# Weight groups' due times, batch 3's transposes and the last 256 tokens' down phase in an attention and two-MLP kernel

## Chip, core and metric

The kernel runs on one core of one Trainium2 chip. The metric is the device time of a run in microseconds (us), as the median over several runs.

## What is computed

The inputs are `x` (8 batches × 8 heads × 512 tokens × 64) and `state` (8 × 8 × 32 × 64), the weights of two MLPs, and the gain `g_ln`. Matrices and results are float32. Cut to what matters:

```python
xread, sread = attention(x -> state), attention(state -> x)      # both ways, per batch and head
y = concat([xread, sread], axis=2)           # 8 x (512 + 32) tokens of 512
# first MLP: W_in 512 x 1024, W_out 1024 x 512
h = y @ moe_w_in
e = exp(h - h.max(-1)); solu = h * e / (e.sum(-1) + 1e-9)
ln = (solu - mean) / sqrt(var + 1e-6) * g_ln
x2 = ln @ moe_w_out
# second MLP: W_in 512 x 2048, W_out 2048 x 512
h = x2 @ moe2_w_in
out = (h * sigmoid(1.702 * h)) @ moe2_w_out
```

## The kernel before, in words

The program has two halves. In the first, attention and the first MLP run batch by batch (8 batches of 512 tokens; the 256 state tokens come as a ninth, smaller batch). In the second, the second MLP runs its up half over all batches and then its down half over all batches. Between the halves the tokens (`x2`) go through DRAM.

Products are made with float32 split into a high and a low part: each full product is three TensorE instructions (hi × hi, lo × hi, hi × lo; lines 422, 423 and 424 in the first MLP, 1010 to 1012 and 1089 to 1091 in the second).

**Transposes.** TensorE contracts over partitions, so tokens have to be turned. Per batch there are two sorts of it. The x transposes turn x for the state's scores (the products on line 571). In `x_T` TensorE turns a block against the identity into PSUM (line 543) and another engine copies it out. In `x_T_dma` four transfers on SyncE lay x out in SBUF so that one VectorE transpose in 32 × 32 blocks (line 533) finishes the work. `XD` is the first batch that takes the second way. The z transposes turn the normalised hidden block `u` for the first MLP's second product. In `z_T` TensorE does it (line 827) and ScalarE and VectorE make the high and low part from PSUM (line 835 for the low part). In `z_turn` VectorE transposes blocks of half the hidden width (line 797, into `zw`), sixteen transfers on SyncE bring them into place (`z`), and ScalarE and VectorE make the two parts in SBUF (line 816 for the low part). From batch `ZB` on, the second half of a batch's hidden width is turned in that way.

**Seven products in place of eight.** The second MLP multiplies 2 × 2 blocks by the scheme with seven products P1 to P7. Its factors are sums of blocks. For the weights, `prepare_up` does it for one group of four blocks (`w3_kq..`; k and q are 0 or 1). `to_f32` first turns raw 64-bit weights into float32 by a chain of integer and float instructions on ScalarE, VectorE (lines 444, 447, 449) and GpSimd (line 451, 1.4 us each). `sums` then makes four sums on VectorE (line 880, names a1 to a4). Seven splits into high and low parts follow (`hi_w3s..`, `lo_w3s..`), and fourteen transfers to DRAM. Four such groups are needed before the up half starts. Three of them are given due times of 205, 255 and 310; the fourth follows later. For the down half `factors_down` loads four blocks of the hidden layer for batch c and makes four sums and seven splits of them. The last 256 tokens are done differently: `down_plain` takes the four plain products with two blocks, one sum and three splits, for two halves of 128 tokens, 192 products of 256 columns in all (lines 1135 to 1137). Then two evacuations of 512 columns (the last one on line 1143) and four stores follow.

**What sets the order.** No engine's order is written out by hand. Every step is handed to a planner (class `Plan`) with a cost, and some with a due time (`key`); a due time goes back along the dependences to the steps ahead of it. The planner simulates the engines and lists each engine's steps: among those that can start, TensorE takes the one with the smallest key and the others the one with the smallest due time. So a smaller due time moves a whole group of steps ahead of others on VectorE, ScalarE, GpSimd and SyncE. Steps that write a new tile wait for a free slot of the tile's kind, and nearly all transfers are issued by SyncE in one order.

Of the kernel before, what the change touches and what calls it, by code (L numbers as in the profile page):

```python
# [343 lines left out]
def attention_solu_gelu(ctx: ExitStack, tc: tile.TileContext, x, state, w1, w2, g_ln, w3, w4, out):  # L344
# [774 lines left out]
    def down_plain(base):  # L1119

        acc = [tl("m", [P, 512], F32, f"W{u}") for u in range(2)]
        gs = [factors_down(B, j, base + j * 4 * PP) for j in range(NM // 2)]
        dst = out.rearrange("(b t) e -> b t e", t=T)
        nb = P // NS
        for u in range(2):
            for j in range(NM // 2):
                for n, (f, i, gi) in enumerate(((0, P1, 0), (0, P2, 1), (1, P7, 0), (1, P3, 2))):
                    def go(e, j=j, n=n, f=f, i=i, gi=gi, u=u):
                        hi, lo = gs[j][gi]
                        o = acc[u]()[:, 256 * f:256 * f + 256]  # L1130
                        cut = slice(u * P, u * P + P)
                        for mi in range(2):
                            wt = W4[i, 2 * j + mi]()
                            first = not j and not mi and not n
                            nc.tensor.matmul(o, hi()[:, mi, cut], wt[:, 0], start=first, stop=False, **OPEN)  # L1135
                            nc.tensor.matmul(o, hi()[:, mi, cut], wt[:, 1], start=False, stop=False, **OPEN)  # L1136
                            nc.tensor.matmul(o, lo()[:, mi, cut], wt[:, 0], start=False, stop=2 * j + mi == NM - 1 and n == 3, **OPEN)  # L1137
                    do(PE(PP / 2), go, [*gs[j][gi], W4[i, 2 * j], W4[i, 2 * j + 1]], [acc[u]],
                       base + (u * 8 + j * 2 + n / 2) * PP)
            o = tl("s", [P, DM], F32, f"os{u}")  # L1140
            due = base + 8 * (u + 1) * PP
            if u:
# [124 lines left out]
```

## Time and profile before

| | before |
|---|---|
| median of 3 runs | 1137.73 us (1136.8 to 1139.35) |
| the profiled execution | 1138.69 us |
| its span in the trace | 1136.9 us |
| TensorE products busy | 1091.8 us, 96% |
| VectorE busy | 811.9 us, 71% |
| ScalarE busy | 636.8 us, 56% |
| GpSimd busy | 257.7 us, 23% |
| granted TensorE clock, mean | 0.984 of full speed |

The span is what the trace covers of an execution. Busy shares are means over the whole program, and it has stages of different kinds: attention and the first MLP up to about 450 us (their last tokens some 25 us longer), then the up half of the second MLP to about 790 us, its down half to the end. Which engine is waited for has to be read stage by stage, from stretches. The granted clock says at what share of full speed TensorE was allowed to run.

### The profile page before, as it was taken

To read this page: it belongs to the slowest core of one execution; us is meant where nothing else is said; L and a number is where in the kernel's file an instruction comes from. 1 tells how busy PE (TensorE), PEld (TensorE's weight loads), DVE (VectorE), ACT (ScalarE), POOL (GpSimd) and SP (SyncE) were. 2 spreads that over 40 slices of the span, in tenths; PEclk is the share of its full clock that TensorE was granted. 3 is DMA by queue.
4 is the path that set the end of the run, shared out by engine and by line. 5 is a ranking of instruction groups with operands and counts; after the bars stand their busy time and mean duration, and the time that the engine had idled before them with its cause. 6 is when DMAs were issued, how large, how long until landed. Compare 5 with 4: busy or idle time off the path is not lost.

```text
span 1136.9 us, 21706 instructions
## 1 busy us (share of the span) xinstructions
PE 1091.8 (96%) x8111; PEld 987.6 (87%) x8111; DVE 811.9 (71%) x1370; ACT 636.8 (56%) x1168; POOL 257.7 (23%) x219
## 2 busy tenths in 40 slices
PE   6799899998999999999999999999999999999998
PEld 2467677776676789999999999999999999999998
DVE  6999677499879946728857755635488888778870
ACT  6686655865867646637756665645244444344430
POOL 3865352455548510501111001000000000000000
PEclk8999899999999999999999999999999999999999
DMA  8213133328663649998677667459944254334511
GB/s 250 56 40 110 40 60 85 104 51 261 135 192 129 194 90 358 350 360 292 232 239 239 240 214 256 175 207 398 383 144 123 66 176 138 119 123 149 178 55 47
DMA packets 216185, 200.67 MB, mean 177 GB/s; under 512 B 111888, under 2 KB 157968, under 8 KB 216080
## 3 DMA queue, kind: packets, MB, share of 16 engines
q1 hardware_dynamic: 215984, 199.16, 55.1%
q8 instruction: 63, 1.03, 0.4%
q14 instruction: 42, 0.34, 0.1%
q10 hardware_dynamic: 96, 0.13, 0.0%
HBM read 112.20 MB, written 82.84 MB: 172 GB/s over the span
## 4 chain that ended last, share of the span: by engine, by line
PE 57%; DVE 1%; DMA 1%; POOL 0%; issue 0%; ACT 0%; POOLq 0%; DVEq 0%; ACTq 0%
PE psum L1089 9%; PE psum L1090 9%; PE psum L1091 9%; PE psum L1010 9%; PE psum L1011 9%; PE psum L1012 9%; PE psum L1137 1%; PE psum L1057 1%; PE psum L1136 1%; PE psum L1058 1%; PE psum L1056 1%; PE psum L1135 1%; DMA w3k_1l<-lo_w3s 0%; DVE lo_x L957 0%; DMA w3k_1h<-hi_w3s 0%
## 5 line engine op out<-in xcount | busy, mean ns | idle before, releaser
L1089 PE MATMUL psum<-w4r,hi_g 128*128 128x256 f32 x896 | 251.8, 281 | 1.7 <-DVE oc L1100 1.7
L1090 PE MATMUL psum<-w4r,hi_g 128*128 128x256 f32 x896 | 251.6, 281 | 0.0
L1091 PE MATMUL psum<-w4r,lo_g 128*128 128x256 f32 x896 | 251.4, 281 | 0.0
L1089 PEld LDWEIGHTS psum<-w4r,hi_g 128*128 128x128 f32 x896 | 169.1, 189 | 1.8 <-ACT hi_g L463 1.8
L1091 PEld LDWEIGHTS psum<-w4r,lo_g 128*128 128x128 f32 x896 | 169.2, 189 | 0.0
L1090 PEld LDWEIGHTS psum<-w4r,hi_g 128*128 128x128 f32 x896 | 169.0, 189 | 0.0
L463 ACT CAST hi_g<-a_g 128x512 fp32r<-128x512 f32 x124 | 75.2, 620 | 120.4 <-DVE a_g L880 79.5
L451 POOL TENSOR_TENSOR w_w<-w_w,raw_w 128x512 uint32<-128x512 uint32 x48 | 68.8, 1439 | 283.7 <-DVE w_w L449 152.4
L422 PE MATMUL psum<-zhi,hi_w 128*128 128x512 f32 (+1 forms) x288 | 116.7, 405 | 2.8 <-DVE zlo L835 1.3
L1022 DVE TENSOR_TENSOR c<-psum,u 128x512 f32<-128x512 f32 x64 | 44.1, 690 | 98.5 <-PE psum L1012 63.8
L424 PE MATMUL psum<-zhi,lo_w 128*128 128x512 f32 (+1 forms) x288 | 111.7, 388 | 0.0
L957 DVE TENSOR_TENSOR lo_g<-a_g,hi_g 128x512 fp32r<-128x512 f32 x128 | 83.8, 685 | 18.3 <-PE psum L1090 9.5
L994 ACT ACTIVATE t<-c 128x512 f32<-128x512 f32 x96 | 60.5, 633 | 51.1 <-DVE c L1022 49.5
L423 PE MATMUL psum<-zlo,hi_w 128*128 128x512 f32 (+1 forms) x224 | 85.7, 382 | 0.1
L957 DVE TENSOR_TENSOR lo_g<-gr,hi_g 128x512 fp32r<-128x512 f32 x104 | 70.8, 684 | 11.0 <-ACT hi_g L463 9.2
L463 ACT CAST hi_g<-gr 128x512 fp32r<-128x512 f32 x104 | 61.4, 618 | 28.2 <-PE psum L1090 14.5
L422 PEld LDWEIGHTS psum<-zhi,hi_w 128*128 128x128 f32 x288 | 55.4, 192 | 19.5 <-issue 4.1
L424 PEld LDWEIGHTS psum<-zhi,lo_w 128*128 128x128 f32 x288 | 55.5, 193 | 11.6
L1010 PE MATMUL psum<-hi_x,w3r_1h 128*128 128x256 f32 x224 | 63.0, 281 | 1.2 <-ACT u L1017 1.2
L1011 PE MATMUL psum<-lo_x,w3r_3h 128*128 128x256 f32 x224 | 63.0, 281 | 0.0
L1011 PE MATMUL psum<-lo_x,w3r_2h 128*128 128x256 f32 x224 | 63.0, 281 | 0.0
L1011 PE MATMUL psum<-lo_x,w3r_0h 128*128 128x256 f32 x224 | 63.0, 281 | 0.0
(256 smaller groups left out, 3104.2 us busy)
## 6 DMA issues: line engine op xcount, KB each, us to landing
g<-t SPq DMA_DIRECT2D x136, 256.0 KB, 2.9
gr<-g SPq DMA_DIRECT2D x136, 256.0 KB, 3.5
w4r<-w4k SPq DMA_DIRECT2D x56, 256.0 KB, 5.2
raw_w<-in_moe_w_in SPq DMA_DIRECT2D x24, 512.0 KB, 5.4
...
```

Of the source, the lines that this page charges most:

```text
L422: nc.tensor.matmul(o, lhi, rhi, start=first, stop=False)
L423: nc.tensor.matmul(o, lhi, rlo, start=False, stop=False)
L424: nc.tensor.matmul(o, llo, rhi, start=False, stop=last)
L451: do(POOL(1.23), lambda e: e.tensor_tensor(u(), u(), raw()[:, :, 0], op=ALU.add), [w, raw], [w], key=due)
L463: e.copy(o, i)
L957: do(DVE(.68), lambda e: e.tensor_tensor(flat_(lo), flat_(t), flat_(hi), op=ALU.subtract), [t, hi], [lo], key=due)
L1010: nc.tensor.matmul(o, wh()[:, k, cut], hi()[:, k, :], start=first and not mi + k, stop=False, **OPEN)
L1011: nc.tensor.matmul(o, wh()[:, k, cut], lo()[:, k, :], start=False, stop=False, **OPEN)
L1012: nc.tensor.matmul(o, wl()[:, k, cut], hi()[:, k, :], start=False, stop=bool(mi and k), **OPEN)
L1089: nc.tensor.matmul(o, hi()[:, mi, cut], wt[:, 0], start=first, stop=False, **OPEN)
L1090: nc.tensor.matmul(o, hi()[:, mi, cut], wt[:, 1], start=False, stop=False, **OPEN)
L1091: nc.tensor.matmul(o, lo()[:, mi, cut], wt[:, 0], start=False, stop=2 * j + mi == NM - 1 and u == 1, **OPEN)
```

## The change

Three things change.

**Batch 3 goes over to the second way of transposing.** `ZB` and `XD` fall from 4 to 3. Batch 3's x transposes are now sixteen transfers and four VectorE transposes; the second half of its z transposes is four VectorE transposes, sixteen transfers and the two parts made in SBUF. TensorE loses 16 transposes of x and 16 of u.

**Two weight groups get smaller due times:** 205 and 255 become 160 and 230. The third keeps 310.

**The last 256 tokens' down phase** takes seven products instead of four times two. `factors_down` now makes four half-size sums for each of four steps j (in tiles `s` and `r`) and four splits, and `down_last` runs 7 × 4 × 6 = 168 products of 256 columns. The results are combined by half-size evacuations, each of which adds an earlier one, as `finish` does it for the other batches. The stores of 128 tokens go out when P4 is in; the other four follow P3.

```diff
-ZB = 4
-XD = 4
+ZB = 3
+XD = 3
...
-            prepare_up(k, q, (205, 255, 310)[n])
+            prepare_up(k, q, (160, 230, 310)[n])
...
-            parts = sums("a", g, f"g{c}_{j}")
-        else:
-            d = tl("s", [P, 512], F32, f"gd{j}")
-            do(SUM, lambda e: e.tensor_tensor(d(), g[0](), g[1](), op=ALU.add), g, [d])
-            parts = [*g, d]
-        return [split2(t, f"g{c}_{j}{i}", None) for i, t in enumerate(parts)]
+            return [split2(t, f"g{c}_{j}{i}", None) for i, t in enumerate(sums("a", g, f"g{c}_{j}"))]
+        s, r = (tl("s", [P, 512], F32, f"gs{i}_{j}") for i in range(2))
...
+        def two(o, i, x, y, op):
+            do(DVE(.4), lambda e: e.tensor_tensor(cut(o, i), cut(*x), cut(*y), op=op), [x[0], y[0]], [o])
+        two(s, 0, (g[0], 1), (g[1], 1), ALU.add)
+        two(r, 0, (s, 0), (g[0], 0), ALU.subtract)
+        two(s, 1, (g[0], 1), (g[0], 0), ALU.subtract)
+        two(r, 1, (g[1], 0), (r, 0), ALU.subtract)
+        return [split2(t, f"g{c}_{j}{i}", None) for i, t in enumerate((*g, s, r))]
...
-    def down_plain(base):
...
+    def down_last(base):
+        gs = [factors_down(B, j, base) for j in range(NM // 2)]
+        place = {P1: (0, 0), P2: (1, 0), P3: (3, 1), P4: (1, 1), P5: (2, 0), P6: (3, 0), P7: (2, 1)}
...
+        order = ((P1, 0), (P6, 1), (P7, 2), (P5, 3), (P2, 4), (P4, 5), (P3, 6))
+        for i, n in order:
+            if not n % 2:
+                acc[n // 2] = tl("m", [P, 512], F32, f"E{n // 2}")
             for j in range(NM // 2):
...
+                do(PE(PP / 2), go, [*gs[j][place[i][0]], W4[i, 2 * j], W4[i, 2 * j + 1]], [acc[n // 2]],
+                   base + (n * 4 + j) * PP / 2)
...
+        x1 = half(P1, None, "px1")
+        u1 = half(P6, x1, "pu1")
+        u2 = half(P7, u1, "pu2")
+        half(P5, u2, None, (1, 1))
+        u3 = half(P5, u1, "pu3")
+        half(P2, x1, None, (0, 0))
+        half(P4, u2, None, (1, 0))
+        store(1)
+        half(P3, u3, None, (0, 1))
+        store(0)
...
-    down_plain(base)
+    down_last(base)
```

Three places show how the order moves. The names end in batch and block numbers: `xn3_0` is block 0 of batch 3's x, `u1_2` block 2 of batch 1's hidden layer, `xT` and `stT` are turned x and state, `v`, `hi_v` and `lo_v` a product of weights and state, `ahi` attention weights.

TensorE, where batch 3's x is transposed (about 119 to 129 us); before:

```order
L423 MATMUL psum_69<-zlo0_7_1267,hi_w2_7_1294 128x512
L424 MATMUL psum_69<-zhi0_7_1247,lo_w2_7_1306 128x512
L543 MATMUL psum_69<-ident_79,xn3_0_1120 128x128 x4
L543 MATMUL psum_69<-ident_79,xn3_1_1138 128x128 x4
L543 MATMUL psum_69<-ident_79,xn3_2_1163 128x128 x4
L543 MATMUL psum_69<-ident_79,xn3_3_1187 128x128 x4
L827 MATMUL psum_69<-ident_79,u1_0_910 128x128
L827 MATMUL psum_69<-ident_79,u1_1_937 128x128
L827 MATMUL psum_69<-ident_79,u1_2_1058 128x128
L827 MATMUL psum_69<-ident_79,u1_3_1228 128x128
```

After:

```order
L423 MATMUL psum_69<-zlo0_7_1247,hi_w2_7_1289 128x512
L424 MATMUL psum_69<-zhi0_7_1234,lo_w2_7_1301 128x512
L571 MATMUL psum_69<-xT3_1_1308,stT3_948 64x512
L571 MATMUL psum_69<-xT3_0_1299,stT3_948 64x512
L422 MATMUL psum_69<-hi_v2_0_0_1323,ahi2_0_1266 128x512
L423 MATMUL psum_69<-lo_v2_0_0_1327,ahi2_0_1266 128x512
L424 MATMUL psum_69<-hi_v2_0_0_1323,alo2_0_1279 128x512
L422 MATMUL psum_69<-hi_v2_0_1_1386,ahi2_0_1266 128x512
L423 MATMUL psum_69<-lo_v2_0_1_1399,ahi2_0_1266 128x512
L424 MATMUL psum_69<-hi_v2_0_1_1386,alo2_0_1279 128x512
L827 MATMUL psum_69<-ident_79,u1_0_910 128x128
L827 MATMUL psum_69<-ident_79,u1_1_937 128x128
```

The four steps on line 543 are gone, and two score steps of batch 3 and six products of batch 2 stand ahead of u1's transposes instead.

VectorE at about 200 to 210 us, in batch 4's attention, where `w_w3_00ij` are blocks of the first weight group and `zw3` is the block of batch 3's z being turned; before:

```order
L602 RECIPROCAL z1_4_1_2162<-z1_4_1_2162 128x16
L783 TENSOR_SCALAR sml3_2_2063<-sml3_2_2063 128x1
L606 STREAM_TRANSPOSE aT4_1_2198<-s1_4_1_2109 128x512
L533 STREAM_TRANSPOSE xT5_2_2212<-xb5_2_2187 128x512
L533 STREAM_TRANSPOSE xT5_3_2220<-xb5_3_2189 128x512
L465 CAST ahi4_1_2234<-aT4_1_2198 128x512
L641 TENSOR_SCALAR sr4_2299<-psum_69,r2_4_0_2008 128x128
L641 TENSOR_SCALAR sr4_2299<-psum_69,r2_4_1_2112 128x128
```

After:

```order
L602 RECIPROCAL z1_4_1_2215<-z1_4_1_2215 128x16
L444 TENSOR_SCALAR w_w3_0000_2193<-w_w3_0000_2193 128x512
L447 TENSOR_SCALAR w_w3_0000_2193<-w_w3_0000_2193 128x512
L444 TENSOR_SCALAR w_w3_0001_2202<-w_w3_0001_2202 128x512
L449 SCALAR_TENSOR_TENSOR w_w3_0000_2193<-raw_w3_0000_2098,w_w3_0000_2193 128x512
L447 TENSOR_SCALAR w_w3_0001_2202<-w_w3_0001_2202 128x512
L606 STREAM_TRANSPOSE aT4_1_2257<-s1_4_1_2124 128x512
L797 STREAM_TRANSPOSE zw3_1_1989<-u3_2_2090 128x512
L880 TENSOR_TENSOR a2_w3_00_2274<-a1_w3_00_2168,w_w3_0000_2193 128x512
L880 TENSOR_TENSOR a3_w3_00_2283<-w_w3_0010_1998,w_w3_0000_2193 128x512
L465 CAST ahi4_1_2292<-aT4_1_2257 128x512
L533 STREAM_TRANSPOSE xT5_0_2328<-xb5_0_2104 128x512
```

Five conversion steps and two sums of the first weight group, and one transpose of batch 3's z, stand among batch 4's steps; before, the group came later.

VectorE near 388 us, where `z6` is batch 6's z, `u7` and `sml7` batch 7's hidden layer and its small values, and `w3..01` the third weight group; before:

```order
L449 SCALAR_TENSOR_TENSOR w_w3_0101_4073<-raw_w3_0101_4022,w_w3_0101_4073 128x512
L880 TENSOR_TENSOR a2_w3_01_4109<-a1_w3_01_3984,w_w3_0100_4060 128x512
L816 SCALAR_TENSOR_TENSOR z6_1_3900<-z6_1_3900,g_sb_81,zhi6_5_4058 128x4x128
L775 SCALAR_TENSOR_TENSOR u7_3_4104,sml7_3_4088<-psum_69,u7_3_4104 128x1024
L880 TENSOR_TENSOR a3_w3_01_4132<-w_w3_0110_3822,w_w3_0100_4060 128x512
L880 TENSOR_TENSOR a4_w3_01_4139<-w_w3_0101_4073,a2_w3_01_4109 128x512
L780 TENSOR_SCALAR sml7_2_4020<-sml7_2_4020 128x1
L780 TENSOR_SCALAR sml7_3_4088<-sml7_3_4088 128x1
L458 TENSOR_TENSOR lo_w3s6_01_4155<-a3_w3_01_4132,hi_w3s6_01_4142 128x512
L816 SCALAR_TENSOR_TENSOR z6_1_3900<-z6_1_3900,g_sb_81,zhi6_6_4081 128x4x128
L816 SCALAR_TENSOR_TENSOR z6_1_3900<-z6_1_3900,g_sb_81,zhi6_7_4090 128x4x128
```

After:

```order
L775 SCALAR_TENSOR_TENSOR u7_2_4065,sml7_2_4042<-psum_69,u7_2_4065 128x1024
L816 SCALAR_TENSOR_TENSOR z6_1_3921<-z6_1_3921,g_sb_81,zhi6_4_4076 128x4x128
L816 SCALAR_TENSOR_TENSOR z6_1_3921<-z6_1_3921,g_sb_81,zhi6_5_4086 128x4x128
L780 TENSOR_SCALAR sml7_2_4042<-sml7_2_4042 128x1
L797 STREAM_TRANSPOSE zw7_1_4116<-u7_0_3900 128x512
L458 TENSOR_TENSOR lo_w3s4_01_4126<-a1_w3_01_3906,hi_w3s4_01_3991 128x512
L771 TENSOR_REDUCE sml7_3_4132<-psum_69 128x1
L816 SCALAR_TENSOR_TENSOR z6_1_3921<-z6_1_3921,g_sb_81,zhi6_6_4112 128x4x128
L783 TENSOR_SCALAR sml7_2_4042<-sml7_2_4042 128x1
L816 SCALAR_TENSOR_TENSOR z6_1_3921<-z6_1_3921,g_sb_81,zhi6_7_4118 128x4x128
L775 SCALAR_TENSOR_TENSOR u7_3_4145,sml7_3_4132<-psum_69,u7_3_4145 128x1024
```

The sums a2 to a4 of the third group no longer stand here; z6_4 to z6_7 now stand ahead of u7_3.

After about 402 us every engine has the same rows in the same order as before, up to the last phase.

## Rows read from the trace of the kernel before

**Rows 1.** Stretches of the span: length, busy us (instructions) by engine, granted clock, DMA.

```profile
50.00:119.00 69.00, 64.56 (x417) 46.80 (x416) 65.91 (x114) 55.66 (x107) 44.94 (x38) 0.98 0.22 62
119.00:129.00 10.00, 6.55 (x28) 5.44 (x27) 6.92 (x14) 5.42 (x9) 6.00 (x7) 0.66 0.31 114
129.00:240.00 111.00, 110.29 (x640) 84.05 (x640) 75.57 (x146) 68.54 (x134) 39.21 (x38) 1.00 0.29 68
240.00:265.00 25.00, 24.26 (x179) 19.43 (x178) 24.50 (x46) 19.50 (x42) 17.79 (x14) 1.00 0.58 141
265.00:328.00 63.00, 57.59 (x301) 42.53 (x300) 54.13 (x95) 43.97 (x82) 30.63 (x28) 0.95 0.70 178
328.00:401.00 73.00, 67.81 (x352) 51.84 (x351) 64.38 (x106) 48.47 (x93) 51.41 (x42) 0.98 0.56 167
401.00:475.00 74.00, 73.56 (x488) 66.70 (x486) 45.88 (x74) 43.93 (x77) 16.41 (x13) 1.00 0.83 268
475.00:1110.00 635.00, 632.61 (x5352) 632.23 (x5353) 433.56 (x703) 319.30 (x564) 23.82 (x17) 1.00 0.61 206
1110.00:1137.00 27.00, 22.93 (x195) 22.72 (x193) 1.38 (x2) 0.60 (x1) 0.00 (x0) 0.97 0.14 39
```

**Rows 2.** In order of time: start, us, instruction [idle before it <- releaser].

```profile
121.44 2.59 PE L543 MATMUL psum<-ident,xn 128*128 128x128 f32 x12 [1.88 <-DVE xs L465]
125.60 1.09 PE L827 MATMUL psum<-ident,u 128*128 128x128 f32 x4 [1.57 <-DVE xT L465]
133.98 1.08 PE L571 MATMUL psum<-xT,stT 128*64 128x512 f32 x4
...
123.03 1.70 DVE L786 TENSOR_SCALAR u<-u,sml 128x1024 f32<-128x1024 f32 x1 [1.40 <-POOL sml L785]
```

**Rows 3.** Line 533 (xT): duration ns min/median/max, first and last start.

```profile
L533 DVE STREAM_TRANSPOSE xT<-xb x16: 666/700/711, 159.6 to 331.1; 128x512 f32<-128x512 f32 x16
```

**Rows 4.** TensorE in order of time, around four transposes of batch 3.

```profile
225.58 0.39 PE L424 MATMUL psum<-zhi,lo_w 128*128 128x512 f32 x1
225.81 0.60 PE L827 MATMUL psum<-ident,u 128*128 128x128 f32 x4
226.17 0.48 PE L422 MATMUL psum<-hi_v,ahi 128*128 128x512 f32 x1
226.49 0.39 PE L423 MATMUL psum<-lo_v,ahi 128*128 128x512 f32 x1
```

**Rows 5.** Two shorter stretches, columns as in rows 1.

```profile
194.45:220.07 25.62, 25.50 (x179) 19.96 (x177) 14.11 (x34) 21.84 (x42) 13.44 (x12) 1.00 0.28 56
390.00:396.00 6.00, 5.26 (x16) 4.19 (x17) 6.00 (x10) 3.23 (x7) 4.72 (x4) 0.72 0.65 242
```

**Rows 6.** Instructions that touch w_w alone, in two stretches, columns as in rows 1.

```profile
248.00:276.00 28.00, 0.00 (x0) 0.00 (x0) 12.20 (x16) 4.45 (x7) 9.68 (x7) 0.99 0.83 251
312.00:346.00 34.00, 0.00 (x0) 0.00 (x0) 11.58 (x17) 3.82 (x6) 8.14 (x6) 0.99 0.63 183
```

**Rows 7.** Line 880 (block sums): duration ns min/median/max, first and last start.

```profile
L880 DVE TENSOR_TENSOR a_g<-gr,gr x64: 678/683/694, 760.9 to 1085.1; 128x512 f32<-128x512 f32 x64
L880 DVE TENSOR_TENSOR a_w<-w_w,a_w x4: 685/1456/1786, 269.0 to 472.5; 128x512 f32<-128x512 f32 x4
```

**Rows 8.** All engines in order of time, at the wait before 390.74.

```profile
388.47 1.66 POOL L451 TENSOR_TENSOR w_w<-w_w,raw_w 128x512 uint32<-128x512 uint32 x1 [0.63 <-DVE w_w L449]
388.92 1.77 DVE L816 SCALAR_TENSOR_TENSOR z<-z,g_sb,zhi 128x512 fp32r<-128x512 f32 x1
390.74 0.50 PE L423 MATMUL psum<-z,hi_w 128*128 128x512 f32 x1 [2.23 <-DVE z L816]
```

**Rows 9.** Line 1137 (last phase): duration ns min/median/max, first and last start.

```profile
L1137 PE MATMUL psum<-w4r,lo_g x64: 276/282/288, 1110.3 to 1132.7; 128*128 128x256 f32 x64
```

**Rows 10.** All engines in order of time, the span's end.

```profile
1132.97 0.69 DVE L1143 TENSOR_SCALAR os<-psum 128x512 f32<-128x512 f32 x1 [21.98 <-PE psum L1137]
1133.69 0.78 SPq L1149 DMA_DIRECT2D out<-os  x2
```

More of the change, by code (lines that the diff above doesn't have):

```diff
@@ L1117, in finish @@
         store(half(P3, u3, "oc12_"), 0, 1)
-    def down_plain(base):
-        acc = [tl("m", [P, 512], F32, f"W{u}") for u in range(2)]
-        gs = [factors_down(B, j, base + j * 4 * PP) for j in range(NM // 2)]
+    def down_last(base):
+        gs = [factors_down(B, j, base) for j in range(NM // 2)]
+        place = {P1: (0, 0), P2: (1, 0), P3: (3, 1), P4: (1, 1), P5: (2, 0), P6: (3, 0), P7: (2, 1)}
+        acc = {}
         dst = out.rearrange("(b t) e -> b t e", t=T)
         nb = P // NS
-        for u in range(2):
-            for j in range(NM // 2):
[L1127 to L1142, printed above, removed]
-                do(DVE(.6), lambda e, o=o, u=u: e.tensor_scalar(o(), acc[u](), 1 / 1.702, None, op0=ALU.mult), [acc[u]], [o],
-                   key=due)
-            else:
-                do(ACT(.5), lambda e, o=o, u=u: e.activation(o(), acc[u](), AF.Copy, scale=1 / 1.702), [acc[u]], [o], key=due)
-            for q in range(nb):
-                def go(e, o=o, u=u, q=q):
-                    e.dma_start(out=dst[u * nb + q, S:T, :], in_=o()[q * NS:(q + 1) * NS, :])
-                do(ACT(.1) if u and q % 2 else DMA(), go, [o], [], key=due + 20, nbytes=P * 512)
@@ new lines, in down_last, with part, go @@
+        o = [tl("s", [P, 2, 256], F32, f"os{u}") for u in range(2)]
+        def part(n, i):
+            n_, c = divmod(n, 2)
+            return acc[n_]()[:, 256 * c:256 * c + 256]
+        order = ((P1, 0), (P6, 1), (P7, 2), (P5, 3), (P2, 4), (P4, 5), (P3, 6))
+        for i, n in order:
+            if not n % 2:
+                acc[n // 2] = tl("m", [P, 512], F32, f"E{n // 2}")
+            for j in range(NM // 2):
+                def go(e, i=i, n=n, j=j):
+                    t, u = place[i]
+                    hi, lo = gs[j][t]
+                    cut = slice(u * P, u * P + P)
+                    for mi in range(2):
+                        wt = W4[i, 2 * j + mi]()
+                        last = j == NM // 2 - 1 and mi == 1
+                        nc.tensor.matmul(part(n, i), hi()[:, mi, cut], wt[:, 0], start=not (j or mi or n % 2), stop=False, **OPEN)
+                        nc.tensor.matmul(part(n, i), hi()[:, mi, cut], wt[:, 1], start=False, stop=False, **OPEN)
+                        nc.tensor.matmul(part(n, i), lo()[:, mi, cut], wt[:, 0], start=False, stop=last, **OPEN)
+                do(PE(PP / 2), go, [*gs[j][place[i][0]], W4[i, 2 * j], W4[i, 2 * j + 1]], [acc[n // 2]],
+                   base + (n * 4 + j) * PP / 2)
@@ new lines, in down_last, with half, view @@
+        places = dict(order)
+        due = base + 14 * PP
+        def half(i, t, name, to=None):
+            n = places[i]
+            if to is None:
+                w = tl("s", [P, 256], F32, name)
+                dst_ = w
+            else:
+                w, dst_ = o[to[0]], None
+            def view():
+                return dst_() if dst_ is not None else w()[:, to[1]]
+            if t is None:
+                do(ACT(.3), lambda e: e.activation(view(), part(n, i), AF.Copy, scale=1 / 1.702), [acc[n // 2]], [w], key=due)
+            else:
+                do(DVE(.4), lambda e: e.scalar_tensor_tensor(out=view(), in0=part(n, i), scalar=1 / 1.702, in1=t(),
+                                                             op0=ALU.mult, op1=ALU.add), [acc[n // 2], t], [w], key=due)
+            return w
@@ new lines, in store, with go @@
+        def store(u):
+            for q in range(nb):
+                def go(e, q=q):
+                    e.dma_start(out=dst[u * nb + q, S:T, :], in_=o[u]()[q * NS:(q + 1) * NS].rearrange("p a e -> p (a e)"))
+                do(ACT(.1) if not u and q % 2 else DMA(), go, [o[u]], [], key=due + 20, nbytes=P * 512)
+        x1 = half(P1, None, "px1")
[4 more added lines that the diff above has]
+        half(P2, x1, None, (0, 0))
```

2 lines of the change are left out of this document (added).

## The prediction, made before the changed kernel ran

> **What bounds the kernel now.** The first view to read is the table of stretches [rows 1]. Its columns after the length are busy time on TensorE's products, its weight loads, VectorE, ScalarE and GpSimd, then the granted clock. From 401 us on TensorE is busy 706 of 709 us up to 1110 us: whatever VectorE does there is hidden, and time falls only if TensorE gets less to do. Ahead of 401 us it is idle 4.4 us of 69 up to 119 us, 3.5 of 10 at 119 to 129, only 0.7 of 111 up to 240, then 0.7 of 25, 5.4 of 63 and 5.2 of 73. In those last three VectorE is busy 98%, 86% and 88% of the time: TensorE waits for VectorE there. The clock is a second price: a granted 0.66 over 10 us is 3.4 us of lost full-speed time, 0.95 over 63 us is 3.2, 0.98 over 73 us is 1.5.
>
> The instruction order shows a rigid end: from about 402 us on, every engine has the same rows in the same order until the last phase. So a microsecond won ahead of 402 us arrives at the end whole, and a microsecond lost does too. The sum is made against the profiled execution, 1138.69 us (span 1136.9), which is 0.96 us above the median of the runs; I apply it to the median, 1137.73.
>
> **1. The last 256 tokens' down phase.** Before, 192 products run from 1110.3 us; the 64 of one line start 22.4 us apart, first to last [rows 9], so a product takes 22.4 / 63 / 3 = 0.1185 us. Seven products of 4 × 6 are 168, 24 fewer: −2.84 us. The last evacuation before the stores took 0.69 us for 512 columns [rows 10]; the changed one has 256, which I put at 0.42 (an estimate, between half and all): −0.27. VectorE gets sixteen half-size sums for four whole ones, and four more splits, some 6 us in all; it is idle 21.98 us ahead of that evacuation [rows 10], and the inputs are loaded before the phase begins. So the sums hide. If they came late, at the worst the whole gain would go. **−3.1 (−3.1 to 0).**
>
> **2. Batch 3's x transposes, 119 to 129 us.** TensorE waits 1.88 us for VectorE at 121.44, runs twelve transposes for 2.59, waits 1.57 at 125.60, and runs the transposes of u1 [rows 2]. In the changed order the x transposes are gone. Ahead of u1 stand two of the score rows (four instructions, 1.08 us, [rows 2]) and six 512-column products, which follow one another in 0.23 us as [rows 4] has it: 2.5 us of work that came later before. What ends the wait then is the normalisation of u1_3 on VectorE, which ended at 123.03 + 1.70 = 124.73 [rows 2]. Ahead of it VectorE gets up to four of the new transposes, 0.70 each [rows 3], and one 0.68 us subtraction more, and it loses 1.67 us of other work: 0 to 1.8 us later. So u1's transposes start at 124.7 to 126.5 instead of 125.60, with 2.5 us already done: a gain of 1.6 to 3.4. The sixteen transfers on SyncE go ahead of others in its queue, but the DMA engines are busy 0.31 here [rows 1]. What could take the gain away is the clock, 0.66 in this stretch: if it falls again and lasts longer, nothing is left. **−2.0 (−3.4 to 0).**
>
> **3. Half of batch 3's z transposes.** They lie in the stretch of 129 to 240 us, where TensorE is 99% busy, so their time counts whole. Four of them took from 225.81 to 226.17 = 0.36 us, and the product behind them came 0.09 us later than its neighbours (0.32 for 0.23) [rows 4]. Four such groups go: 4 × 0.45 = **−1.8 (−1.8 to −1.4)**. VectorE gets four transposes of 0.70 instead and is busy 75.57 of 111 us there [rows 1]; the sixteen transfers find DMA engines busy 0.29. If that cover failed, TensorE would wait for z, which belongs to the next term.
>
> **4. The first weight group into 187 to 222 us.** Its due time falls from 205 to 160, and its instructions move from about 250 to 274 us to among those of 187 to 222. VectorE's share of a group is 16 to 17 instructions, 12.20 or 11.58 us [rows 6]. The stretch that takes it, 194.45 to 220.07, is 25.62 us long and TensorE is busy 25.50 of them; VectorE is busy 14.11 [rows 5]. Added: 12.5 for the group, 2.1 for three z transposes; gone: two instructions of some 0.7 that move elsewhere, 1.4. That makes 14.1 + 12.5 + 2.1 − 1.4 = 27.3 us where 25.6 are there. One end is no cost, since what does not fit can slide into the relieved stretch behind. The other is 2.0 of overflow, as much again for waits in the order on GpSimd and ScalarE, and one fall of the clock (1.7, as 0.72 over 6 us gives it [rows 5]): 5.7. I take the overflow, since the share of VectorE is what the rows show. **+2.0 (0 to +5.7).**
>
> **5. 240 to 265 us.** Relieved of that group's start, VectorE is no longer busy 24.50 of 25 us [rows 1]; TensorE's idle time there goes. **−0.7 (−0.7 to 0).**
>
> **6. 265 to 328 us.** The rest of the first group leaves, some 6 us, and the second group (due 255 to 230, from 312 to 344 us to among 267 to 300) comes in with 11.6: VectorE from 54.13 to some 59.7 of 63. TensorE is idle 5.4 us. Nothing in the rows says which waits vanish. Below, the lost clock of 3.2 us could come back; above, one more wait as that at 390.74 with its clock would cost 3.9. **0 (−3.2 to +3.9).**
>
> **7. 328 to 401 us.** The second group is gone from here: VectorE falls from 64.38 to about 53 to 59 of 73 (something of the third group draws closer). The longest wait is 2.23 us at 390.74, for batch 6's z, whose low part took 1.77 us beside a GpSimd instruction on a weight block and stood behind the third group's sums [rows 8]. The clock after it was 0.72 over 6 us, 1.7 us lost [rows 5]. In the changed order two of those sums stand earlier, and z6's parts stand ahead of u7_3. I take that one wait with its clock, 2.23 + 1.7. The far end is the stretch's whole idle time and lost clock, 5.2 + 1.5; the near end is 1 us, if another z is late next. **−3.9 (−6.7 to −1.0).**
>
> **Sum.** −3.1 − 2.0 − 1.8 + 2.0 − 0.7 + 0 − 3.9 = −9.5, that is 1137.7 − 9.5 = **1128.2 us**. All terms at their best give −18.9, about 1119; all at their worst +7.2, about 1145.
>
> **Rivals.** *The stalls only move.* VectorE does no less in all; weight sums taken from 312 to 344 us are done in stretches that are full too. Then term 4 comes out at its far end, 3.7 more than in the sum, and term 6 at +3.0, a wait and most of a fall of the clock: 1128.2 + 6.7 = about **1134.9**. For it: VectorE 86 to 98% busy around 240 to 401 [rows 1]. Against: VectorE is idle 35 of the 111 us from 129 to 240. Chance 0.20.
>
> *Slower: the group's two-input operations stretch beside GpSimd.* The weight sums of line 880 took 1456 ns in the middle and 1786 at most, where the same form later takes 683 [rows 7]. GpSimd is busy 13.44 of the 25.62 us of term 4's stretch before anything is added [rows 5], and a group adds 8 to 10 us to it [rows 6]. If nine VectorE instructions there take 1 us more each (0.8 to 1.1 by those rows), VectorE needs 36.3 us in 25.6: TensorE waits 10.7 and loses 1.7 to the clock, 12.4 instead of 2.0. The same in term 6 adds 3.9 + 1.7, term 7's gain staying: 1128.2 + 10.4 + 5.6 = about **1144**. It decides once VectorE's work in that stretch passes some 33 us, where terms 1 to 3 are eaten. Against it: a group's 12.20 and 11.58 us already hold such stretching, with GpSimd busy 9.68 of 28 us on the group itself [rows 6]. Chance 0.08. The Trainium skill, "SBUF — State Buffer", section "Who interferes with whom", has a rule for this: a VectorE instruction with two inputs in SBUF contends with a GpSimd instruction that reads SBUF, and one of them blocks. The rows agree (1456 to 683 ns for one form); by that rule alone each such instruction would wait for a whole GpSimd one, 1.66 us [rows 8], and this rival would be the forecast.
>
> *The waits of 265 to 328 us go too.* Terms 6 at −3.2 and 7 at −6.7: 1128.2 − 6.0 = about **1122**. For it: the order there is looser for z. Against: VectorE has more to do there. Chance 0.12.
>
> *The last phase gives nothing*, its sums coming late for the second product, which starts 24 × 0.1185 = 2.8 us into the phase: **1131.3**. Chance 0.05.
>
> **How the numbers follow.** The forecast has 0.55. The range leaves out the slower rival, half of the first's upper edge and the deepest part of the third: 1121 to 1136. A measurement of this kernel can tell 0.2%, 2.3 us, from no change. The forecast, the third and the fourth rival are faster; of the first rival's 0.20, 0.06 falls within 0.2%. So faster 0.86, same 0.06, slower 0.08.
>
> **What would show it.** In the profile of the changed kernel: products of the last phase ending about 19.9 us after they start (term 1); TensorE's idle time in 119 to 129 us under 2 us (2); VectorE's busy time between about 190 and 215 us near the length of that stretch, with TensorE's idle time there of 0 to 2 us (4), while well over 2 means the slower rival; no wait of over 2 us for z ahead of the stretch that answers to 401 (7). The start of the rigid part should come about 6 us earlier, and the last phase 3 more. The forecast is wrong if TensorE's idle time and lost clock between 129 and 401 us don't fall by some 2 us net.

## The result, and the profile after

The changed kernel took 1125.66 us (median of 6 runs, 1124.97 to 1129.33); the kernel before, run beside it, 1138.11. The ratio is 0.9899, with a 95% interval of 0.9885 to 0.9913: 11.5 us less, by 9.9 to 13.1. The forecast was 1128.2 us, 9.5 less, in a range of 1121 to 1136. So the number was right. The experiments show that most of its terms were not.

The page of the changed kernel: busy time and share of the span of TensorE and VectorE, in a span of 1124.3 us (before 1136.9).

```profile
PE 1080.0 (96%) x8055; PEld 976.9 (87%) x8055; DVE 825.2 (73%) x1398; ACT 637.8 (57%) x1171; POOL 258.7 (23%) x218
```

TensorE was busy 1091.8 us before, so its idle time is 1136.9 − 1091.8 = 45.1 us before and 1124.3 − 1080.0 = 44.3 after. **The waits as a whole hardly shrank.** What shrank is TensorE's busy time, by 11.8 us. To see where, I cut both traces at the same instructions of TensorE. In the rows, `u` is a hidden block, `sml` its small values, `e2t` the exponentials of the state's scores and `sr` the state's scaled result, per batch. First the kernel before: start and end of the stretch, its length, busy us of TensorE's products, its weight loads, VectorE, ScalarE, GpSimd, the granted clock, DMA.

```profile
117.25:138.57 21.32, 17.87 (x80) 13.88 (x80) 15.10 (x26) 11.20 (x20) 8.55 (x9) 0.84 0.15 54
138.57:194.54 55.97, 55.38 (x327) 42.58 (x325) 40.29 (x80) 31.35 (x64) 20.46 (x21) 1.00 0.32 68
194.54:228.75 34.21, 34.09 (x219) 25.96 (x217) 19.66 (x39) 27.33 (x51) 13.62 (x12) 1.00 0.41 107
253.94:280.12 26.18, 22.64 (x97) 16.34 (x94) 24.30 (x34) 16.61 (x29) 16.97 (x13) 0.93 0.87 273
280.12:327.46 47.34, 44.72 (x255) 33.79 (x253) 40.18 (x78) 35.57 (x66) 22.24 (x21) 0.96 0.64 143
327.46:399.10 71.64, 66.44 (x346) 50.78 (x345) 64.21 (x106) 49.01 (x94) 50.15 (x40) 0.98 0.58 171
```

The same stretches of the changed kernel:

```profile
118.52:134.53 16.01, 13.96 (x63) 10.05 (x64) 13.05 (x27) 11.39 (x20) 9.33 (x10) 1.00 0.28 91
134.53:190.32 55.79, 55.22 (x326) 42.66 (x325) 41.45 (x75) 32.82 (x67) 19.61 (x20) 1.00 0.32 77
190.32:231.21 40.89, 35.03 (x220) 25.94 (x218) 38.00 (x64) 30.88 (x58) 26.60 (x21) 1.00 0.63 179
256.08:275.89 19.81, 19.81 (x96) 15.33 (x94) 15.05 (x26) 13.48 (x24) 5.77 (x6) 1.00 0.90 205
275.89:324.91 49.02, 43.62 (x256) 32.48 (x253) 45.06 (x78) 36.92 (x68) 26.96 (x21) 1.00 0.67 175
324.91:388.91 64.00, 63.84 (x347) 49.94 (x345) 55.44 (x98) 44.41 (x90) 43.94 (x36) 1.00 0.49 136
```

By these pairs: −5.3 us where batch 3's x is turned, −0.2 in the next stretch, **+6.7 where the first weight group now lies**, −6.4 where it lay, +1.7, and −7.6 in the last. The stretch left out here (229 to 254 us before) gives −0.3. From then on the order is the same, and the trace is 10 us ahead up to the last phase, which adds 2.9. VectorE's busy time shows the move: 19.66 to 38.00 us in the third pair, 24.30 to 15.05 in the fourth.

In the third stretch TensorE, idle 0.1 us before, now waits 5.9. The largest of these waits, in order of time (start, us, instruction, [idle before it <- releaser]):

```profile
199.04 0.50 PE L422 MATMUL psum<-hi_w1s,sthi 128*128 128x512 f32 x1 [1.71 <-DVE zlo L835]
212.36 0.51 PE L422 MATMUL psum<-hi_w1s,sthi 128*128 128x512 f32 x1 [2.13 <-DVE sr L641]
222.17 0.33 PE L827 MATMUL psum<-ident,u 128*128 128x128 f32 x1 [1.46 <-POOL u L786]
```

And VectorE's instructions of the first group there run long (groups of that stretch: busy us, mean ns | idle before):

```profile
L465 DVE CAST hi_w3s<-w_w 128x512 fp32r<-128x512 f32 x3 | 3.5, 1162 | 0.0
L458 DVE TENSOR_TENSOR lo_w3s<-w_w,hi_w3s 128x512 fp32r<-128x512 f32 x2 | 2.3, 1155 | 0.0
L880 DVE TENSOR_TENSOR a_w<-a_w,w_w 128x512 f32<-128x512 f32 x1 | 1.8, 1759 | 0.0
L465 DVE CAST hi_w3s<-a_w 128x512 fp32r<-128x512 f32 x2 | 0.8, 424 | 0.0
```

One cast form takes 1162 ns on the mean where its like takes 424, and a sum 1759 where [rows 7] has 683 for the plain case. The planner that set this order counts a low part (line 458) at 0.6 us on VectorE, whatever runs beside it.

The span's end, which answers to [rows 10]: the last evacuation has half the columns and takes 0.42 us, as estimated.

```profile
1120.41 0.42 DVE L1174 SCALAR_TENSOR_TENSOR os<-psum,pu 128x256 f32<-128x256 f32 x1 [2.09 <-PE psum L1155]
1120.87 0.89 ACTq L1181 DMA_DIRECT2D out<-os  x2
```

### The profile page after: what moved, and what is told of

It is laid out like the page before. It is cut to its first block, busy times and chain, and to the rows that moved or that the text cites. A ratio compares the mean times of both kernels' runs of the same rounds, so it can differ in the third digit from the quotient of the medians.

```text
span 1124.3 us, 21689 instructions
## 1 busy us (share of the span) xinstructions
PE 1080.0 (96%) x8055; PEld 976.9 (87%) x8055; DVE 825.2 (73%) x1398; ACT 637.8 (57%) x1171; POOL 258.7 (23%) x218
## 4 chain that ended last, share of the span: by engine, by line
PE 75%; DVE 13%; issue 3%; SPq 3%; POOL 3%; DMA 2%; ACT 1%; DVEq 0%; POOLq 0%; ACTq 0%
PE psum L1098 9%; PE psum L1100 9%; PE psum L1099 9%; PE psum L1010 9%; PE psum L1011 9%; PE psum L1012 9%; PE psum L422 5%; PE psum L423 5%; PE psum L424 4%; DVE w_w L449 1%; DVE w_w L444 1%; SPq L529 1%; POOL lo_w3s L458 1%; DVE w_w L447 1%; DVE u L775 1%
## 5 line engine op out<-in xcount | busy, mean ns | idle before, releaser
L422 PE MATMUL psum<-zhi,hi_w 128*128 128x512 f32 (+1 forms) x288 | 113.9, 395 | 1.3 <-DVE zlo L835 0.6
L957 DVE TENSOR_TENSOR lo_g<-gr,hi_g 128x512 fp32r<-128x512 f32 x104 | 71.0, 685 | 11.8 <-ACT hi_g L463 9.2
L423 PE MATMUL psum<-zlo,hi_w 128*128 128x512 f32 (+1 forms) x208 | 78.3, 376 | 0.2
L424 PEld LDWEIGHTS psum<-zhi,lo_w 128*128 128x128 f32 x288 | 54.1, 188 | 11.8 <-DVE lo_w L458 0.4
L1010 PE MATMUL psum<-hi_x,w3r_2h 128*128 128x256 f32 x224 | 63.0, 281 | 0.0
```

What stands on the lines that cost most here:

```text
L422: nc.tensor.matmul(o, lhi, rhi, start=first, stop=False)
L423: nc.tensor.matmul(o, lhi, rlo, start=False, stop=False)
L424: nc.tensor.matmul(o, llo, rhi, start=False, stop=last)
L957: do(DVE(.68), lambda e: e.tensor_tensor(flat_(lo), flat_(t), flat_(hi), op=ALU.subtract), [t, hi], [lo], key=due)
L1010: nc.tensor.matmul(o, wh()[:, k, cut], hi()[:, k, :], start=first and not mi + k, stop=False, **OPEN)
```

## Experiments

Twelve kernels, each against the kernel before on the same chip. Since the median of the kernel before moved between 1136.0 and 1138.1 us from one session to the next, differences are taken from the ratios (a thousandth is 1.14 us).

| kernel | median us | ratio to before (95%) | us against before |
|---|---|---|---|
| the change | 1125.66 | 0.9899 (0.9885 to 0.9913) | −11.5 |
| e1, last phase alone | 1133.83 | 0.9973 (0.9959 to 0.9988) | −3.1 |
| e2, batch 3's transposes alone | 1139.83 | 1.0027 (1.0017 to 1.0037) | +3.1 |
| e3, due times alone | 1138.89 | 1.0014 (1.0003 to 1.0025) | +1.6 |
| e5, change, first due 205 | 1139.61 | 1.0020 (1.0008 to 1.0032) | +2.3 |
| e6, change, second due 255 | 1130.48 | 0.9940 (0.9927 to 0.9954) | −6.8 |
| e7, change, `XD` 4 | 1130.82 | 0.9945 (0.9932 to 0.9957) | −6.3 |
| e8, change, `ZB` 4 | 1130.22 | 0.9939 (0.9925 to 0.9952) | −6.9 |
| e10, change, casts on ScalarE | 1125.66 | 0.9896 (0.9880 to 0.9911) | −11.8 |
| e11, change, first due 180 | 1126.12 | 0.9898 (0.9882 to 0.9914) | −11.6 |
| e12, change, first due 140 | 1125.11 | 0.9895 (0.9876 to 0.9913) | −11.9 |
| e13, change, low parts on VectorE | 1125.55 | 0.9892 (0.9875 to 0.9909) | −12.3 |
| e15, first due 140 and low parts on VectorE | 1122.07 | 0.9877 (0.9861 to 0.9894) | −14.0 |

### The three parts alone (e1, e2, e3)

e1 keeps only the last phase; its edit to the changed kernel:

```diff
-ZB = 3
-XD = 3
+ZB = 4
+XD = 4
...
-            prepare_up(k, q, (160, 230, 310)[n])
+            prepare_up(k, q, (205, 255, 310)[n])
```

> The kernel before with only the last phase changed. Theory of the sum (each term stands for itself, the order ahead of the last phase being the same): 2.9 to 3.1 us less than before, about 1135.1; TensorE's products of the last phase spread over 19.9 us. Theory that what precedes decides: less than 1 us. Falls of the granted clock ahead of the last phase as in the kernel before (at about 88, 125, 276, 310 and 393 us).

−3.1 us, as the sum had it. Its order ahead of the last phase is that of the kernel before, and so are most of its waits; yet its profile differs from [rows 1] in the clock. Kernel before (length, TensorE busy, granted clock, DMA):

```profile
274.00:278.00 4.00, 3.41 (x10) 0.67 1.01 328
310.00:314.00 4.00, 4.00 (x14) 0.64 0.08 18
```

The same stretches of e1, and in a second view, in order of time, the waits ahead of them:

```profile
274.00:278.00 4.00, 3.88 (x16) 1.00 0.96 308
310.00:314.00 4.00, 4.00 (x21) 1.00 0.00 0
```

```profile
272.47 0.66 PE L827 MATMUL psum<-ident,u 128*128 128x128 f32 x4 [1.14 <-ACT stT L463]
274.12 0.50 PE L422 MATMUL psum<-zhi,hi_w 128*128 128x512 f32 x1 [0.99 <-DVE u L775]
307.04 0.59 PE L648 MATMUL psum<-ident,sr 128*128 128x128 f32 x2 [2.09 <-DVE sr L641]
```

Before, the same three waits were 1.14, 1.01 and 2.04 us, and the clock fell to 1.2 GHz behind them. Here it did not. The trace of e1 was 0.5 us ahead of that of before at 272 us and 2.1 at 278, still 2.1 at 306 and 3.6 at 311. So a fall costs some 1.5 us, and one order with nearly the same waits has it in one execution and not in another. The expectation that the falls stay was wrong for three of five (the one at 88 us was missing too).

e2 and e3 make the other two edits in the kernel before:

```diff
-ZB = 4
-XD = 4
+ZB = 3
+XD = 3
```

> The kernel before with only batch 3's transposes changed. Theory of the sum: terms 2 and 3, 2.0 + 1.8 = 3.8 us less, about 1134.3. Theory A, that much of the gain is the clock: the stretch of 117 to 139 us gives 4 to 5 us, the fall of the clock at 125 us is gone, those at about 276, 310 and 393 us are still there; 5 to 7 us less, about 1132. Theory B, that stalls only move: VectorE's extra transposes turn up as new waits of TensorE further on, and the whole gives under 1.5 us.

```diff
-            prepare_up(k, q, (205, 255, 310)[n])
+            prepare_up(k, q, (160, 230, 310)[n])
```

> The kernel before with only the two due times changed. Theory of the sum: terms 4 to 7, 2.6 us less, about 1135.5. Theory A (clock): TensorE's idle time up to 400 us is the same within 2 us, but the falls of the granted clock at about 276, 310 and 393 us are gone, worth some 4.5 us; 3 to 6 us less, about 1133.5; the fall at 125 us is still there. Theory B (stalls only move, the clock with them): within 1.5 us of before.

Each alone makes the kernel slower, by 3.1 and 1.6 us, against every theory of a gain; only the rival of moving stalls comes near, and it had them at no change. The three parts alone add up to −3.1 + 3.1 + 1.6 = +1.6 us; together they give −11.5. **Thirteen microseconds are in no part by itself, but in their meeting.** On batch 3's x e2 gains some 5 us: its trace is 3.9 us behind that of before at 117 us (batch 2's `sr`) and 1.4 ahead at 148 (batch 3's second scores). Where does it lose them? First at 273.85 us. Its TensorE row, and VectorE in order of time before it:

```profile
273.85 0.59 PE L422 MATMUL psum<-zhi,hi_w 128*128 128x512 f32 x1 [4.17 <-DVE u L775]
```

```profile
267.90 1.41 DVE L880 TENSOR_TENSOR a_w<-a_w,w_w 128x512 f32<-128x512 f32 x1
269.23 1.75 DVE L880 TENSOR_TENSOR a_w<-w_w,w_w 128x512 f32<-128x512 f32 x1
270.90 1.75 DVE L880 TENSOR_TENSOR a_w<-w_w,a_w 128x512 f32<-128x512 f32 x1
272.57 1.21 DVE L775 SCALAR_TENSOR_TENSOR u<-psum,u 128x1024 f32<-128x1024 f32 x1
```

Batch 5's hidden block stands behind three of the first group's sums on VectorE, which take 4.9 us in place of 2.0 (3 × 0.68). In the 20 us around it, first e2 and then the changed kernel (columns as in the tables of stretches):

```profile
255.00:275.00 20.00, 11.80 (x57) 8.94 (x56) 19.86 (x26) 13.01 (x22) 14.25 (x11) 0.98 0.74 239
```

```profile
255.00:275.00 20.00, 20.00 (x96) 15.76 (x94) 15.24 (x27) 13.80 (x24) 5.91 (x7) 1.00 0.89 202
```

VectorE is busy 19.86 of 20 us in e2 and TensorE idle 8.2; with the group gone, TensorE is busy all 20.

That is not the whole of e2's loss. TensorE takes batch 7's first scores (line 571) at 324.8 us, where the kernel before has them at 326.4, so the trace is 1.6 us ahead again there. What it loses then goes at two later waits, where the kernel before has one of 1.15 us and none; VectorE is busy 19.86 of the 20 us from 350 to 370, and the clock falls behind the second wait:

```profile
344.28 0.33 PE L621 MATMUL psum<-ident,e2t 128*128 128x128 f32 x1 [3.79 <-ACT e2t L583]
366.35 0.47 PE L827 MATMUL psum<-ident,u 128*128 128x128 f32 x1 [3.34 <-POOL u L786]
```

e3 moves the group away but has nothing to set against what it costs in its new place. There, 190 to 231 us:

```profile
190.00:231.00 41.00, 36.15 (x222) 27.12 (x221) 39.45 (x65) 30.16 (x56) 28.89 (x23) 0.96 0.53 157
```

After that stretch its trace is some 7 us later than that of before (TensorE takes batch 4's `sr` at 221.2 us for 214.0). It wins this back bit by bit, with a wait of 2.9 us for `sr` of batch 6 at 315 us on the way, and ends level in the profiled pair (spans 1136.1 and 1136.9). The falls of the clock at 276, 310 and 393 us are gone from its trace, as theory A of its expectation had it, with one new at 218 us; a gain of 3 to 6 us did not come with that.

### One due time at a time (e5, e6, e11, e12)

Each changes one number of the changed kernel, for the first or the second group:

```diff
-            prepare_up(k, q, (160, 230, 310)[n])
+            prepare_up(k, q, (205, 230, 310)[n])   # e5
+            prepare_up(k, q, (160, 255, 310)[n])   # e6
+            prepare_up(k, q, (180, 230, 310)[n])   # e11
+            prepare_up(k, q, (140, 230, 310)[n])   # e12
```

> The changed kernel with the first group's due time back at 205 (205, 230, 310). In the changed kernel the stretch of 190 to 231 us is 6.7 us longer than in the kernel before, and that of 256 to 276 us 6.4 us shorter. If the first due time pays for itself (theory of the sum: +2.0, then gains behind it): 3 to 6 us slower than the changed kernel, about 1130, with the first group's work and TensorE's waits back at 240 to 280 us. If the loss at 190 to 231 us was in vain: within 1.5 us of the changed kernel, or faster.

> The changed kernel with the second group's due time back at 255 (160, 255, 310). Theory of the sum (terms 6 and 7 belong to the second group): some 3.9 us slower than the changed kernel, about 1129.5, with waits of TensorE back between 310 and 390 us. Theory that the first due time with batch 3's transposes makes the whole gain: within 1.5 us of the changed kernel.

With the first group's old due time the change is lost whole, 13.8 us (from −11.5 to +2.3), more than either theory had. The first wait of e2 is back:

```profile
270.40 0.79 PE L422 MATMUL psum<-zhi,hi_w 128*128 128x512 f32 x1 [4.16 <-DVE u L775]
```

A longer one follows it, and it comes from the second group, whose due time e5 leaves at 230. Three of that group's sums hold VectorE from 309.4 to 314.3 us, batch 7's turned x, which TensorE waits for, comes behind them, and the clock is at half speed from 316 to 326 us:

```profile
317.86 1.98 PE L571 MATMUL psum<-xT,stT 128*64 128x512 f32 x4 [6.22 <-DVE xT L533]
```

```profile
309.36 1.58 DVE L880 TENSOR_TENSOR a_w<-a_w,w_w 128x512 f32<-128x512 f32 x1
310.86 1.77 DVE L880 TENSOR_TENSOR a_w<-w_w,w_w 128x512 f32<-128x512 f32 x1
312.56 1.74 DVE L880 TENSOR_TENSOR a_w<-w_w,a_w 128x512 f32<-128x512 f32 x1
```

In the changed kernel these three sums start at 292.2 to 294.5 us. So e5 does more than bring one group back: the first group, late, also pushes the second later. No run tells the two losses apart.

With the second group's old due time 4.7 us are lost, near the 3.9 of the sum. From about 290 to 335 us the trace runs in front of the changed kernel's (batch 6's `sr` at 303.3 us for 307.2); then it falls back, in part at this wait and the fall of the clock behind it (336 to 340 us, TensorE busy throughout):

```profile
335.50 0.33 PE L621 MATMUL psum<-ident,e2t 128*128 128x128 f32 x1 [2.75 <-ACT e2t L583]
```

```profile
336.00:340.00 4.00, 4.00 (x13) 0.57 0.49 188
```

Is 160 a lucky number, or does anything do that brings the first group's sums ahead of about 250 us?

> The changed kernel with the first group's due time at 180 instead of 160, between the old and the new value. Theory that what counts is that the first group's sums are out of the way before about 250 us, where batch 5's hidden block (u5_0) waited 4.2 us behind them: within 2 us of the changed kernel, about 1126, and no wait over 2 us at 255 to 275 us. Rival, that 160 happens to give a lucky order: 4 us or more slower.

> The changed kernel with the first group's due time at 140: its VectorE work then lies at about 175 to 215 us instead of 187 to 231. Theory of room (VectorE is idle by 15 us of the 56 at 139 to 195 us in the kernel before, by 14.6 of the 34 behind): within 2 us of the changed kernel, the loss of 6.7 us at 190 to 231 us partly moved ahead. Rival (lucky order): 4 us or more slower.

Both are within 0.5 us of the changed kernel, so the rival of a lucky order falls for the first group. At 180 the trace has a wait of 3.3 us at 243, where the changed kernel has one of 1.15 at 246, at 140 one of 2.9 at 303; neither has the 4.2 us wait at 270.

### One transpose at a time (e7, e8)

```diff
-XD = 3
+XD = 4   # e7
...
-ZB = 3
+ZB = 4   # e8
```

> The changed kernel with XD back at 4, so batch 3's x is turned by TensorE, its z still half by VectorE. Theory that the x transposes stand for themselves: 4 to 6 us slower than the changed kernel, about 1130.5, all of it between 117 and 139 us (a wait of 1.9 us and one of 1.6 to 1.9 us back, with the fall of the clock behind them), the rest of the trace shifted rigidly. Theory of interaction: the loss also grows behind 190 us, together over 8 us.

5.2 us (from −11.5 to −6.3), inside the expected 4 to 6 and where it was expected: by 126 us its trace has lost 5 us on the changed kernel, and it stays 3 to 5 behind from there. Its rows are those of [rows 2] again:

```profile
120.92 2.21 PE L543 MATMUL psum<-ident,xn 128*128 128x128 f32 x12 [1.88 <-DVE xs L465]
125.08 1.09 PE L827 MATMUL psum<-ident,u 128*128 128x128 f32 x4 [1.95 <-DVE xT L465]
```

> The changed kernel with ZB back at 4, so batch 3's z is turned by TensorE, its x still by VectorE. Theory of the sum (term 3): 1.4 to 1.8 us slower than the changed kernel, about 1127.3. Theory of interaction (the order behind 215 us falls in another way): 4 us or more to either side, with waits of over 2 us between 220 and 330 us that the changed kernel does not have.

4.6 us, not 1.4 to 1.8, and not in the place of the transposes: up to 260 us its trace lies within about 1 us of the changed kernel's. It falls back at 306 to 324 us, with a fall of the clock behind this wait, which the changed kernel has not:

```profile
311.05 0.47 PE L648 MATMUL psum<-ident,sr 128*128 128x128 f32 x1 [2.99 <-DVE sr L641]
```

Ahead of batch 6's `sr` VectorE there works off two low parts of the second weight group (1.59 us each), a low part and a cast of `v` (1.42, 1.52); in the changed kernel one low part and one step of batch 6 stand in their place. That is the planner's choice some 50 us behind the edit. How one leads to the other was not settled.

### GpSimd beside VectorE (e10, e13, e15)

```diff
-            for h, t in zip("hl", split(t, f"w3s{i}_{k}{q}", due)):
+            for h, t in zip("hl", split(t, f"w3s{i}_{k}{q}", due, high=(("act", .52),))):   # e10
+            for h, t in zip("hl", split(t, f"w3s{i}_{k}{q}", due, low=(("dve", .6),))):   # e13
```

> The changed kernel with the high parts of the weight groups made by ScalarE alone; in the changed kernel VectorE makes five of them at 190 to 231 us, three at 1162 ns each and two at 424. Theory that VectorE's stretched instructions cost the 6.7 us that this stretch is longer: VectorE's busy time there falls from 38.0 by about 4, TensorE's idle time from 5.9 to 2 to 4, and the kernel gets 2 to 4 us faster, about 1122.5. Rival: ScalarE (busy 30.9 of 40.9 us there) becomes late instead: no gain or slower.

The six casts go to ScalarE (`high` is a new argument of `split`). No change in time, where 2 to 4 us were expected. The stretch of 190 to 231 us, as in the table of the changed kernel above:

```profile
190.32:231.21 40.89, 36.40 (x222) 27.73 (x220) 35.93 (x60) 33.18 (x63) 24.14 (x19) 0.96 0.58 170
```

VectorE's busy time falls by 2.1 us there, not 4, and TensorE's idle time from 5.9 to 4.5, while the mean granted clock is 0.96 there, not 1.00. TensorE takes batch 4's `sr` 5.0 us earlier than in the changed kernel (211.5 us for 216.5), batch 6's 5.0 later (312.2 for 307.2), and batch 7's within 1: three waits of 2.3, 2.8 and 1.7 us, at 221, 254 and 299, each with a fall of the clock behind it, stand in place of others. So these casts were a cost where they stood, and taking them away did not shorten the whole.

> The changed kernel with the low parts of all four weight groups made by VectorE alone; before, GpSimd makes 21 of 28, at some 1.4 to 1.7 us each, while VectorE's instructions beside it stretch (0.42 to 1.2 or 1.5 us, 0.68 to 1.2 or 1.8). Theory of contention: 21 instructions of 0.69 us more on VectorE (14.5 us) are paid back by what no longer stretches, VectorE's busy time over the whole grows by less than 8 us, and the kernel stays within 2 us or gets faster. Rival (VectorE's work counts at its plain length): VectorE's busy time grows by 14 us, TensorE waits 3 to 8 us more, 1129 to 1133.

GpSimd's 21 low parts of the weight groups go to VectorE. The lines of the low parts on VectorE, in the changed kernel and then in e13 (ns min/median/max, first and last start):

```profile
L458 DVE TENSOR_TENSOR lo_w3s<-a_w,hi_w3s x5: 691/1564/1797, 219.8 to 465.0; 128x512 fp32r<-128x512 f32 x5
L458 DVE TENSOR_TENSOR lo_w3s<-w_w,hi_w3s x2: 673/1155/1637, 210.1 to 218.3; 128x512 fp32r<-128x512 f32 x2
```

```profile
L458 DVE TENSOR_TENSOR lo_w3s<-a_w,hi_w3s x16: 673/682/693, 218.5 to 465.6; 128x512 fp32r<-128x512 f32 x16
L458 DVE TENSOR_TENSOR lo_w3s<-w_w,hi_w3s x12: 627/684/1107, 198.2 to 463.8; 128x512 fp32r<-128x512 f32 x12
```

And e13's page:

```profile
PE 1081.5 (96%) x8055; PEld 979.1 (87%) x8055; DVE 830.2 (74%) x1418; ACT 638.9 (57%) x1175; POOL 225.3 (20%) x194
```

VectorE got 21 instructions of 0.69 us more, 14.5 us, and is busy only 830.2 − 825.2 = 5.0 us longer. Not all of the missing 9.5 us is stretching that went away: busy time counts the overlap of one instruction with the next once, and added up one by one VectorE's instructions grew by 9.1 us, so that 5.4 us of the 14.5 were made up for, by less stretching and in part by casts and copies that ScalarE took over. GpSimd does 33 us less. The theory of contention holds in direction, the rival's 14 us do not come.

That it is GpSimd that stretches them shows in the changed kernel's trace itself. Of the 176 sums on line 880 the 160 that overlap no GpSimd instruction in time take 676 to 694 ns, and the 16 that do take 678 to 1812. VectorE's transposes of x (line 533), which read one input, take 658 to 711 ns beside GpSimd and 660 to 705 without. The Trainium skill, "SBUF — State Buffer", section "Who interferes with whom", has the rule: a VectorE instruction with two inputs in SBUF contends with a GpSimd instruction that reads SBUF, and so can casts, by a mode with two ports. The trace agrees for the sums and low parts (682 to 1564 ns) and for the casts (424 to 1162).

Each of due 140 and low parts on VectorE alone left the time as it was. Both together (e15):

```diff
-            for h, t in zip("hl", split(t, f"w3s{i}_{k}{q}", due)):
+            for h, t in zip("hl", split(t, f"w3s{i}_{k}{q}", due, low=(("dve", .6),))):
...
-            prepare_up(k, q, (160, 230, 310)[n])
+            prepare_up(k, q, (140, 230, 310)[n])
```

> The changed kernel with the first due time at 140 and the weight groups' low parts made by VectorE alone, both at once; each alone was within 0.6 us of the changed kernel. With 140 the trace was 5 to 8 us ahead up to 300 us and lost it at a wait of 2.9 us for batch 6 at 303 us and a fall of the clock; without GpSimd's low parts VectorE's instructions stretch less there. Theory that VectorE's stretching makes the wait at 303 us: the lead of 140 stays, 3 to 5 us faster than the changed kernel, about 1121.5. Rival (the wait only moves): within 2 us of the changed kernel, about 1125.

```profile
PE 1078.8 (96%) x8055; PEld 976.7 (87%) x8055; DVE 826.2 (74%) x1417; ACT 640.4 (57%) x1177; POOL 220.5 (20%) x193
```

1122.07 us (1121.14 to 1123.72), the fastest of all; TensorE is idle 40.9 us of 1119.7. The longest wait near 303 us is 2.1 us, not 2.9, no fall of the clock follows it, and of the trace's lead of some 8 us on the changed kernel at 300 us about 4 are kept. Against the changed kernel the ratio is 2.2 thousandths lower with intervals that overlap (up to 0.9894 here, from 0.9885 there). The two were not run side by side, so a gain of some 2.5 us is likely but not settled.

## Why the prediction was right, point by point

- **What bounds the kernel; the rigid end.** Right. From about 402 us on the traces run parallel: 10 us ahead there (6 were forecast), 9.7 at the start of the last phase.
- **Term 1, the last phase, −3.1.** Right: −3.1 in e1, −2.9 in the pair of traces. The products' starts spread over 19.7 us (1100.35 to 1120.09). The rival that it gives nothing is out.
- **Term 2, x transposes, −2.0 (−3.4 to 0).** Too small: 5.2 us in e7, −5.3 in the trace, beyond the range. The wait did shrink as argued, but only from 3.5 to 2.1 us. The larger part is in busy time, 17.87 to 13.96: the sixteen transposes, and the clock, whose 0.66 in [rows 1] stood in the term only as a risk. That this loss could be *won back* was left out, though the same rows price it at 3.4 us.
- **Term 3, z transposes, −1.8.** Wrong in kind. "TensorE is 99% busy, so the time counts whole" was read from a stretch that the rest of the change was about to fill: with the first group in it, TensorE waits 5.9 us there, and transposes taken from it gain nothing on the spot (e8). The 4.6 us that they are worth arise 50 us later, in the planner's order.
- **Term 4, the first group's new place, +2.0 (0 to +5.7).** Too small: +6.7 in the trace. VectorE's load there rose by 18.3 us, where I had 13.2. The 27.3 us of the working over 25.6 give 1.7 of overflow, and not the 2.0 of the sum. The 5.1 us more on VectorE have three sources: instructions on `w_w` run longer, 14.1 us for 16, where I had 12.5 (1.6); [rows 6], which counts `w_w` alone, leaves out three splits of block sums (1.5); and two transposes of x came into the stretch, where I had two instructions leaving it (2.8). Small steps take 0.8 off again. Stretching beside GpSimd, which I had as the slower rival at 0.08, is in the 14.1: TensorE's wait of 5.9 us there is beyond the 2 us that I named as its sign. The mechanism of that rival is real; the 12.4 us that it gave this stretch were too much.
- **Terms 5 to 7, the relieved stretches, −4.6 in all.** Far too small: −0.3 − 6.4 + 1.7 − 7.6 = −12.6, the last of them beyond its far end of −6.7. In [rows 8] I took one wait with its clock; in the trace TensorE's idle time from 325 to 389 us fell from 5.2 to 0.2 us, and no fall of the clock is left ahead of the last phase after 50 us.
- **The sum.** −9.5 for −11.5 (−12.6 in the pair of traces), since term 4 was 4.7 us too low and terms 2 and 5 to 7 were 11.3 too high, with term 3 out by 1.8 on its spot and the trace 1.3 behind up to 118 us. It came right by cancelling. The step that failed is the sum itself: adding parts that share VectorE. Alone, the parts are worth +1.6 us.
- **The rival that the stalls only move** was right on the stalls (45.1 to 44.3 us of idle time) and wrong on the time, for it had no place for busy time. The sign named for a wrong forecast was idle time plus lost clock between 129 and 401 us; in the stretches behind batch 3's x it fell by 4 us, but by the clock alone: the idle part rose from 12.1 to 13.1 us, and the lost clock went from 5.1 to nothing. Of the 11.8 us by which busy time fell, the last phase's 24 products are 2.8, the transposes of x some 2.8 (0.60 and 2.21 us in e7) and those of z 1.8; the remaining 4.4 I put down to the clock. This last is an account, not an experiment. The profiled pair flatters it: over all runs the mean granted clock gives 15.3 us lost before (62 runs, 0.981 to 0.991) and 10.9 after (6 runs, 0.988 to 0.992), while the two profiles have 18.2 and 9.0. Against it stands e11: as fast as the changed kernel, it loses 15.5 us by the same count (4 runs, 0.982 to 0.989), as much as the kernel before. How much of the gain is the clock stays open.
